# Two steps joined per turn of one TensorE loop, with the feed-forward weights and both query products loaded ahead of the attention steps

## The chip, the cores and the metric

One core of a Trainium2 chip, with float32 data throughout. The metric is the device time of one execution in microseconds; of the kernel before three runs are shown, with a median of 374.54 us. A core has five engines that run their own instruction streams: TensorE (PE in the profile; its weight loads are PEld), VectorE (DVE), ScalarE (ACT), GpSimd (POOL) and SyncE (SP). SP issues nearly all loads here; 16 DMA engines carry them out.

## The reference

One token of each of two sequences passes a layernorm, then an attention over a cache of 4096 positions and, beside it, a gated feed-forward; the product of both is added to the input.

```python
B, Sq, D = 2, 1, 448
Hq, Hkv, Sk, Dh = 16, 8, 4096, 256      # caches: (B, Hkv, Sk, Dh)
...
x = A_x
xn = _layernorm(x, axis=-1)
q = (xn @ wq) split into 16 heads; two query heads share one K/V head
s = softmax(q k^T / 16) v, joined over the heads, @ wo
g = silu(((xn w_gate) * (xn w_up)) @ w_down)     # F = 1792
return x + s * g
```

The caches are 2 x 67 MB and the weights some 24 MB, each read once; the output has 896 numbers.

## The kernel before, in words

A *step* is one K/V head of one sequence: 16 steps, numbered i = 2 x head + sequence. For each, K and V are 128 partitions x 8192 floats (4096 KB each). `scores` (lines 461-467) multiplies the query with K, `softmax` (503-505) takes the maximum over everything, the exponential and a transpose into `pT`, and `values` (516-521) multiplies it with V into the PSUM bank `o`.

Loads. There are two large buffers, `ring`, of 128 x 16384 floats, and one, `slot`, for weights (128 x 13440). `plan` lists the loads (lines 293-301) and `issue(n)` puts the next n on SP's queue (270-288). A ring load brings V of a step with K of the next (`vk[i]`, 8192 KB); a weight load brings wq0, then w_gate with w_up (`wgu`), w_down with wq1 (`wdq`), and `wo`. A load into a buffer that has been used waits on SP until TensorE has read the last of the old contents, and since SP issues in order, everything behind it waits too. What is issued is carried out in order.

Start. `issue(3)` on line 302 puts wq0 (with a small load wqx), K of step 0 and V0 with K1 in the queue with no wait. VectorE computes the layernorm and TensorE turns it into `xnT` and `xf`. `query(0)` (562) multiplies with wq0: `rows` (385-407) runs 12 matmuls over the first 384 rows of the weight, and for the last 64 rows of w_q half of the columns come in pieces, some of them from wqx, a tile of 16 partitions (`xeT`, lines 356-361, 397-405). All steps up to 6 are written out (568-581), and between them `ffn_in` (after step 1's softmax), `ffn_out` (step 3) and `query(1)` (step 4), each when its weights have come through the one slot.

Loop. Steps 6 to 13 are four turns of a loop on TensorE (`Flow.loop`, lines 119-149, and 203-207): TensorE's instructions of a turn are emitted once, and their waits become counting gates; the other engines' instructions are written out. In the second step of each turn `hold` (592-594) runs a 128x512 product twice that nobody reads.

Joining. Each step leaves `o` as four partial sums per head; `ob` keeps eight of them. `gather` sums the softmax totals (`total`) and the partial outputs (`combine`) with small matmuls, and `join` divides and transposes into `oT0` (steps 0-5, after step 5) and `oT1` (steps 6-13, after the loop). `project` multiplies with `wo`. The last two steps and the last part of wo, which comes behind V15 in the last loads, follow by hand (611-650).

`LEAD` (32, 154-155) is a number of semaphore increments on VectorE at the start that nobody waits for.

Of the kernel before, what the change touches and what calls it, by code (L numbers as in the profile page):

```python
# [4 lines left out]
AF = mybir.ActivationFunctionType  # L5
OP = mybir.AluOpType
# [14 lines left out]
GROUPS = 3  # L21
EARLY = 4 * GROUPS
LATE = 24
PART = 14 * (D + 512)
HALF = D - 384
SIDE = 16
COLS = 384
CUT = 256 + (512 - COLS) // 2
NS = HALF // SIDE
EPS = 1e-5  # L30
START = B * GROUPS
LEAD = 52
# [198 lines left out]
def gated_decode_block(nc, x, first, vk, last0, last1, wq0, wqx, wdq, wo, wgu, out):  # L231
# [7 lines left out]
    class Ring:  # L239
# [14 lines left out]
        ("mx", [1, NT, W], 1), ("ob", [128, 8, 512], 1))}  # L254
# [15 lines left out]
    def issue(n=1):  # L270
        for names, src, cuts in todo[:n]:
            weight = names[0].startswith("w")
            if weight:
                t = slot()
            else:
                t = ring()
            width = ROW if not weight else src.shape[1] // len(names)
# [6 lines left out]
            if names == ["wq0"]:  # L284
                at = src.shape[1]
                loaded["wqx"] = t[:SIDE, at:at + NS * COLS]
                SP.dma_start(loaded["wqx"], wqx[:, :4])
        del todo[:n]

    def plan(names, src, cuts=None):  # L290
        todo.append((names.split(), src, cuts or [0, src.shape[1]]))

    plan("wq0", wq0)
    plan("k0", first)
    weights = {0: ("wg wu", wgu), 2: ("wd wq1", wdq), 5: ("wo", wo)}
    for i in range(LAST):
        plan(f"v{i} k{i + 1}", vk[i])
        if i in weights:
            plan(*weights[i])
    plan(f"k{LAST + 1} v{LAST}", last0, [0, ROW, 2 * ROW])  # L300
    plan(f"v{LAST + 1} wo2", last1, [0, 6144, ROW, *(ROW + i * D for i in (5, 7, 8))])
    issue(3)
# [43 lines left out]

    oT1 = sbuf([128, HKV - 1 - GROUPS, 2, REP, W], "oT1")
    spare = oT1.rearrange("p g d r m -> p (g d r) m")

    xf = spare[:, NK:NK + 2]  # L350
# [4 lines left out]

    xeT = spare[:SIDE, NK + 2:NK + 2 + NS]
    pt = bank()
    for j in range(NS):
        at = 384 + j * SIDE
        PE.transpose(pt[:SIDE, B * j:B * (j + 1)], xn[:, at:at + SIDE], ident[:B, :B])  # L360
    copies(xeT, pt[:SIDE, :NS * B])

# [22 lines left out]
    def rows(ps, w, n, extra=None):  # L385
# [8 lines left out]
        def last(a, i):  # L394
            PE.matmul(ps[64 * a:64 * (a + 1), :n], xf.rearrange("p a j -> p (a j)"), block(i), start=False, stop=True)

        if extra is not None:
            last(1, 12)
            at = 13 * n
            PE.matmul(ps[W:2 * W, :CUT], xf[:, 0], w[:, at:at + CUT], start=False, stop=False)  # L400
            PE.matmul(ps[W:2 * W, CUT:n], xf[:, 1], w[:, at:at + n - CUT], start=False, stop=True)
            PE.matmul(ps[:W, COLS:n], xf[:, 1], w[:, at + n - CUT:at + CUT], start=False, stop=False)
            for j in range(NS):
                PE.matmul(ps[:W, :COLS], xeT[:, j, :], extra[:, j * COLS:(j + 1) * COLS], start=False, stop=j == NS - 1)
            return
        for a in range(2):
            last(a, 12 + a)
# [4 lines left out]
    def query(h):  # L412
        ps = bank()
        rows(ps, loaded[f"wq{h}"], 512, None if h else loaded["wqx"])
# [55 lines left out]
    su = sbuf([128, N], "su")  # L470

    def place(i):
        g, b = divmod(i, B)
        n = HKV - 1 - GROUPS
        return b * GROUPS + g if i < START else START + b * n + g - GROUPS if i < LAST else i

# [14 lines left out]
    def exponential(i, s, m, mx):  # L491
        sm = bank("sm")
        PE.transpose(sm[:, 128:129], mx.rearrange("p c j -> p (c j)"), one)
        DVE.tensor_scalar(m[:, 1:2], sm[:, 128:129], -1.0 / 16, None, op0=OP.mult)
        p = work["p"]()
        ACT.activation(p, s, AF.Exp, bias=m[:, 1:2], scale=1.0 / 16, accum_out=su[:, place(i):place(i) + 1])
        return p
# [9 lines left out]
    over = sbuf([128, N], "over")  # L507
    copy = Ring("qc", [128, 2, W], 2)

    def total(lo, hi, add):  # L510

        sm = bank("sm")
        PE.matmul(sm[:, :hi - lo], add.rearrange("p a r j -> p (a r j)"), su[:, lo:hi], start=True, stop=True)
        DVE.reciprocal(over[:, lo:hi], sm[:, :hi - lo])
# [8 lines left out]
    def combine(ob, n):  # L523

        cb = bank("cb")
        src = ob.rearrange("p s (e d c k) -> p s e d c k", e=2, d=2, c=NT)
        for e in range(2):
            for c in range(NT):
                PE.matmul(cb[W * c:W * (c + 1), :n * 64], add_blocks[:, e].rearrange("p r j -> p (r j)"),
                                 src[:, :n, e, :, c, :], start=e == 0, stop=e == 1)  # L530
        return cb

    def divide(cb, lo, hi):
        n = hi - lo
        t = work["h"]()
        DVE.tensor_tensor(t[:, :n * 64].rearrange("p (s k) -> p s k", s=n),
                                cb.rearrange("p (s k) -> p s k", s=n),
                                over[:, lo:hi, None].to_broadcast([128, n, 64]), op=OP.mult)
        return t[:, :n * 64]
# [5 lines left out]
    def turn(oT, cb, g, b, n):  # L545
        DVE.transpose(oT[:, g:g + n, :, :, DUP * b:DUP * (b + 1)].rearrange("p g d r j -> p (g d) r j"), cb)

    def heads(oT, i, first):
        return oT[:, i // 4 - first, i % 2, i % 4 // 2]

    def project(oT, first, lo, hi):
        for i in range(lo, hi):
            t = i % NT
            PE.matmul(wide[W * t:W * (t + 1), :D], heads(oT, i, first), loaded["wo"][:, i * D:(i + 1) * D],
# [9 lines left out]
    oT0 = sbuf([128, GROUPS, 2, REP, W], "oT0")  # L564
    oT2 = sbuf([128, 1, 2, REP, W], "oT2")
    s = scores(0, query_of(0), two())
    issue(2)
    for i in range(START):
        p = softmax(i, s)
        if i == 1:  # L570
            ffn_in()
        if i == 3:
            ffn_out()
        if i == 4:
            query(1)
        o = bank("o")
        values(i, p, o)
        s = scores(i + 1, query_of(i + 1), two())
        if i + 1 < START:
            issue(1 if i + 2 == START else 1 + (i + 1 in weights))  # L580
        DVE.tensor_copy(ob[:, place(i)], o)

    def gather(lo, hi):
        total(lo, hi, add_head)
        return combine(ob, hi - lo)

    def join(oT, cb, lo, hi):
        n = (hi - lo) // B
        for b in range(B):
            turn(oT, divide(cb[:, b * n * 64:(b + 1) * n * 64], lo + n * b, lo + n * (b + 1)), 0, b, n)  # L590

    def hold(p):

        PE.matmul(bank("cb"), ident, p[:, 0], start=True, stop=True)

    join(oT0, gather(0, START), 0, START)
    for first in range(START, LAST, 2):
        flow.turn = first
        issue(2)
        for i in (first, first + 1):  # L600
            p = softmax(i, s)
            if i > first:
                hold(p)
                hold(p)
            o = bank("o")
            values(i, p, o)
            DVE.tensor_copy(ob[:, place(i) - START], o)
            q = copy()
            ACT.copy(q, query_of(i + 1))
            s = scores(i + 1, q, two())  # L610
    flow.turn = None
    issue(2)
    m = peak(s)
    cb = gather(START, LAST)
# [3 lines left out]
    join(oT1, cb, START, LAST)  # L618
# [3 lines left out]
    project(oT0, 0, 0, EARLY)  # L622
    m = peak(late)
    project(oT1, GROUPS, EARLY, EARLY + NT)
# [6 lines left out]
    project(oT1, GROUPS, EARLY + NT, LATE)  # L631
    t = work["h"]()
    ACT.copy(t, wide[:, :D])
    total(14, 16, add_step)
    ACT.activation(ob[:, 6], o, AF.Copy, scale=over[:, 14:15])
# [5 lines left out]
    ACT.activation(ob[:, 7], o, AF.Copy, scale=over[:, 15:16])  # L641
    cb = combine(ob[:, 6:], B)
    DVE.transpose(oT2[:, 0].rearrange("p d r (b j) -> p b d r j", b=B), cb[:, :B * 64].rearrange("p (b d r j) -> p b d r j", b=B, d=2, r=REP))
    for i in range(LATE, NC):
        project_last(acc, heads(oT2, i, 7) if i >= 28 else heads(oT1, i, GROUPS), i)
# [55 lines left out]
```

## Time and profile before

| what | number |
|---|---|
| three runs | 374.32, 374.54, 374.59 us |
| profiled execution: span from first to last instruction | 373.3 us |
| median of the runs less that span | 1.24 us |
| TensorE busy | 201.8 us (54%) |
| VectorE busy | 74.1 us (20%) |
| ScalarE busy | 27.8 us (7%) |
| SP's load queue, share of 16 DMA engines | 98.5% |
| read from memory | 158.54 MB |

The profile does not give the profiled execution a time of its own beside its span, so the span is set against the median of the runs: 1.24 us lie outside of it.

How to read the rows: a timeline row has its start in us from the span's start, its length in us (for a row "x32" from the first instruction to the end of the last), engine, line, operation, tile written <- tiles read (buffer numbers left out), count, and in brackets how long the engine had been idle and who ended that. Every instruction passes through one helper, so all of them carry its line (L227 before, L220 in the change); they are told apart by their tiles. A 128x512 float32 matmul is two records, so "x32" are 16 matmuls. In a windows row, after the stretch and its length come the busy time and count of TensorE, the granted TensorE clock (1.00 is full), the busy share of the 16 DMA engines and the GB/s. A packet's whole share is put where it ended, so a short window can show more than 1.00. SPq rows are the issue of a DMA, not its transfer.

### The profile page before, as it was taken

To read this page: it belongs to the slowest core of one execution; us is meant where nothing else is said; L and a number is where in the kernel's file an instruction comes from. 1 tells how busy PE (TensorE), PEld (TensorE's weight loads), DVE (VectorE), ACT (ScalarE), POOL (GpSimd) and SP (SyncE) were. 2 spreads that over 40 slices of the span, in tenths; PEclk is the share of its full clock that TensorE was granted. 3 is DMA by queue.
4 is the path that set the end of the run, shared out by engine and by line. 5 is a ranking of instruction groups with operands and counts; after the bars stand their busy time and mean duration, and the time that the engine had idled before them with its cause. 6 is when DMAs were issued, how large, how long until landed. Compare 5 with 4: busy or idle time off the path is not lost. (4 is left out here: it accounts for less than half of the span.)

```text
span 373.3 us, 3175 instructions
## 1 busy us (share of the span) xinstructions
PE 201.8 (54%) x1416; PEld 58.6 (16%) x1416; DVE 74.1 (20%) x114; ACT 27.8 (7%) x52; POOL 2.4 (1%) x14
## 2 busy tenths in 40 slices
PE   0782449081736084817403667285609470948976
PEld 0220112020101021202100122022202120212223
DVE  2103040103030013030310212122211221030620
ACT  1101010001021001010100000101000101010120
POOL 0100000000000000000000000000000000000000
PEclk9988596677686589886955959686957896776999
DMA  8999999999999999999999999999999999999995
GB/s 329 437 471 400 444 457 435 421 437 400 444 427 428 451 435 430 428 426 433 449 428 428 435 449 409 442 449 421 435 421 449 435 428 442 435 393 432 442 406 240
DMA packets 3921, 158.73 MB, mean 425 GB/s; under 512 B 566, under 2 KB 696, under 8 KB 840
## 3 DMA queue, kind: packets, MB, share of 16 engines
q1 hardware_dynamic: 3908, 158.59, 98.5%
q8 instruction: 8, 0.13, 0.1%
q10 hardware_dynamic: 4, 0.00, 0.0%
q14 instruction: 1, 0.01, 0.0%
HBM read 158.54 MB, written 0.06 MB: 425 GB/s over the span
## 5 line engine op out<-in xcount | busy, mean ns | idle before, releaser
L227 PE MATMUL o<-ring,pT 128*32 128x512 f32 x480 | 76.6, 797 | 101.0 <-DMA ring<-vk 54.2
L227 PEld LDWEIGHTS o<-ring,pT 128*32 128x32 f32 x480 | 19.0, 142 | 153.5 <-issue 97.1
L227 DVE COPY ob<-o 128x512 f32<-128x512 f32 x14 | 9.7, 692 | 168.4 <-PE o L227 168.4
L227 ACT ACTIVATE p<-s,m 128x1024 f32<-128x1024 f32 x16 | 17.8, 1113 | 303.1 <-DVE m L227 303.1
L227 PE MATMUL s<-ring,qT 128*32 128x512 f32 x256 | 30.8, 622 | 1.1 <-DVE qT L227 1.1
L227 PE MATMUL s<-ring,qc 128*32 128x512 f32 x256 | 29.0, 592 | 0.0
L227 DVE TENSOR_REDUCE m<-s 128x1 f32<-128x1024 f32 x16 | 19.5, 1220 | 41.2 <-PE s L227 41.2
L227 DVE STREAM_TRANSPOSE pT<-p 128x1024 f32<-128x1024 f32 x15 | 18.7, 1245 | 19.1 <-ACT p L227 19.1
L227 PE MATMUL cb<-pT,ident 128*128 128x512 f32 x16 | 14.8, 1081 | 11.4 <-PEq L179 11.4
L227 PE MATMUL s<-slot,xnT 128*32 128x512 f32 (+1 forms) x96 | 14.6, 757 | 3.7 <-DMA slot<-wgu 3.7
L227 PE MATMUL sm<-ident,m 128*1 128x128 f32 x16 | 4.3, 270 | 21.0 <-PEq L179 12.9
L227 DVE TENSOR_REDUCE mx<-sm 1x128 f32<-1x512 f32 x16 | 10.9, 679 | 7.9 <-PE sm L227 7.9
L227 PEld LDWEIGHTS s<-ring,qc 128*32 128x32 f32 x256 | 9.0, 110 | 18.6 <-issue 18.6
L227 PEld LDWEIGHTS s<-ring,qT 128*32 128x32 f32 x256 | 8.2, 114 | 20.8 <-issue 20.7
L227 PE MATMUL sm<-one,mx 1*128 1x1 f32 x16 | 3.3, 209 | 12.3 <-PEq L179 6.9
L227 PE MATMUL s<-slot,hT 128*32 128x448 f32 x28 | 5.6, 911 | 4.4 <-DMA slot<-wdq 4.4
L227 PE MATMUL s<-slot,oT 16*32 16x384 f32 (+5 forms) x28 | 8.0, 521 | 0.0
L227 PEld LDWEIGHTS cb<-pT,ident 128*128 128x128 f32 x16 | 4.7, 324 | 15.8 <-issue 15.8
L227 PEld LDWEIGHTS sm<-ident,m 128*1 128x1 f32 x16 | 1.3, 79 | 34.8 <-issue 20.4
L227 PE MATMUL s<-ident,pT 2*128 2x2 f32 (+1 forms) x8 | 0.7, 203 | 10.7 <-DVE pT L227 10.7
L227 PEld LDWEIGHTS s<-slot,xnT 128*32 128x32 f32 x96 | 3.3, 137 | 12.9 <-issue 9.1
L227 PE MATMUL wide<-slot,oT 128*32 128x448 f32 x48 | 4.9, 539 | 0.0
(65 smaller groups left out, 58.2 us busy)
## 6 DMA issues: line engine op xcount, KB each, us to landing
ring<-last SPq DMA_DIRECT2D x2, 4096.0 KB, 26.7
slot<-wdq SPq DMA_DIRECT2D x1, 6720.0 KB, 45.6
slot<-wgu SPq DMA_DIRECT2D x1, 6272.0 KB, 33.7
slot<-wo SPq DMA_DIRECT2D x1, 5376.0 KB, 38.1
ring<-first SPq DMA_DIRECT2D x1, 4096.0 KB, 20.6
slot<-wq SPq DMA_DIRECT2D x1, 3488.0 KB, 11.2
ring<-last SPq DMA_DIRECT2D x1, 3072.0 KB, 21.4
ring<-last SPq DMA_DIRECT2D x1, 1120.0 KB, 24.1
```

The costliest lines, as they stand in the source:

```text
L227: self.flow.record(self.engine, lambda: method(out, *args, **kw), writes, reads, name == "dma_start")
```

## The change

Seven things change together.

- Loads: the order is now wq0 into ring buffer 1, wgu into the slot, wdq into ring buffer 0, K of step 0 behind wq0 in ring buffer 1 (`behind`), and these four are issued at once. V0 with K1 (ring buffer 0) and V1 with K2 (ring buffer 1) are issued with the first turn of the loop, and wo behind them.
- `ffn_in`, `ffn_out` and `query(1)` run straight behind `query(0)`, and the scores of step 0 behind them.
- The loop has seven turns, steps 0 to 13, instead of four.
- Each turn ends with the join of its two steps: `total`, `combine`, one division, one transpose. `oT0` and `oT1` become one tile `oT`, and `ob`, `su` and `over` hold two steps.
- `hold` goes.
- wqx goes: the last 64 rows of w_q are folded onto 128 partitions, as those of w_gate, w_up and wq1 already were, and `query(0)` ends with two 64-column matmuls. wq0 grows from 3488 to 3584 KB.
- `LEAD` is 0.

```diff
-    plan("wq0", wq0)
-    plan("k0", first)
-    weights = {0: ("wg wu", wgu), 2: ("wd wq1", wdq), 5: ("wo", wo)}
+    def behind():
+        return ring.bufs[1][:, WQ:]
+
+    plan("wq0", lambda: ring.bufs[1], wq0)
+    plan("wg wu", slot, wgu)
+    plan("wd wq1", lambda: ring.bufs[0], wdq)
+    plan("k0", behind, first)
     for i in range(LAST):
-        plan(f"v{i} k{i + 1}", vk[i])
-        if i in weights:
-            plan(*weights[i])
...
-    issue(3)
+        plan(f"v{i} k{i + 1}", ring, vk[i])
+        if i == 1:
+            plan("wo", slot, wo)
...
+    issue(4)
...
-        if extra is not None:
-            last(1, 12)
...
-            return
         for a in range(2):
-            last(a, 12 + a)
+            PE.matmul(ps[64 * a:64 * (a + 1), :n], xf.rearrange("p a j -> p (a j)"), block(12 + a), start=False, stop=True)
...
     query(0)
     ob = work["ob"]()
...
+    ffn_in()
+    ffn_out()
+    query(1)
     s = scores(0, query_of(0), two())
-    issue(2)
-    for i in range(START):
...
-    join(oT0, gather(0, START), 0, START)
-    for first in range(START, LAST, 2):
+    for first in range(0, LAST, B):
         flow.turn = first
         issue(2)
-        for i in (first, first + 1):
+        if first == 0:
+            flow.turn = None
+            issue()
+            flow.turn = first
+        for i in range(first, first + B):
             p = softmax(i, s)
-            if i > first:
-                hold(p)
-                hold(p)
             o = bank("o")
             values(i, p, o)
-            DVE.tensor_copy(ob[:, place(i) - START], o)
+            DVE.tensor_copy(ob[:, i % B], o)
             q = copy()
             ACT.copy(q, query_of(i + 1))
             s = scores(i + 1, q, two())
+        total(add_head)
+        cb = combine(ob)
+        t = work["h"]()[:, :B * 64]
+        DVE.tensor_tensor(t.rearrange("p (s k) -> p s k", s=B), cb.rearrange("p (s k) -> p s k", s=B),
+                          over[:, :, None].to_broadcast([128, B, 64]), op=OP.mult)
+        turn(oT, first // B, t)
     flow.turn = None
     issue(2)
     m = peak(s)
-    cb = gather(START, LAST)
```

The queue of SP before, from its start; `first` is K of step 0, `vk` a load of V and K, and a repeated form stands once with its count.

```order
L227 DMA slot<-wq 128x6976
L227 DMA slot<-wqx 16x1x1536
L227 DMA ring<-first 128x8192
L227 DMA ring<-vk 128x16384
L227 DMA slot<-wgu 128x12544
L227 DMA ring<-vk 128x16384 x2
L227 DMA slot<-wdq 128x13440
L227 DMA ring<-vk 128x16384 x3
```

The same place in the change:

```order
L220 DMA ring<-wq 128x7168
L220 DMA slot<-wgu 128x12544
L220 DMA ring<-wdq 128x13440
L220 DMA ring<-first 128x8192
L220 DMA ring<-vk 128x16384 x2
L220 DMA slot<-wo 128x10752
L220 DMA ring<-vk 128x16384 x12
```

The two weight loads moved ahead of K of step 0, and wdq from the slot into a ring buffer, so that the first `vk` load now comes behind it in the same buffer.

TensorE before, from step 3's transposes of the maximum to step 4's values: `s<-slot,hT` and `s<-h,add_head` are `ffn_out`, `s<-slot,xnT 32x512` with the row below it is `query(1)`, `o` rows are `values`, `s<-ring,qT` rows `scores`, and `sm` rows the transposes of the maximum.

```order
L227 MATMUL sm<-ident,m 1x128
L227 MATMUL sm<-one,mx 128x1
L227 MATMUL s<-slot,hT 32x448 x14
L227 MATMUL s<-h,add_head 32x112 x4
L227 MATMUL o<-ring,pT 32x512 x16
L227 MATMUL s<-ring,qT 32x512 x16
L227 MATMUL sm<-ident,m 1x128
L227 MATMUL sm<-one,mx 128x1
L227 MATMUL s<-slot,xnT 32x512 x12
L227 MATMUL s<-slot,oT_17 64x512 x2
L227 MATMUL o<-ring,pT 32x512 x16
```

The same products in the change, from `ffn_in`'s last rows to the first turn of the loop:

```order
L220 MATMUL s<-slot,oT 64x448 x2
L220 MATMUL s<-ring,hT 32x448 x14
L220 MATMUL s<-h,add_head 32x112 x4
L220 MATMUL s<-ring,xnT 32x512 x12
L220 MATMUL s<-ring,oT 64x512 x2
L220 MATMUL s<-ring,qT 32x512 x16
L198 UNCONDITIONAL_BRANCH
L220 MATMUL sm<-ident,m 1x128
L220 MATMUL sm<-one,mx 128x1
L220 MATMUL o<-ring,pT 32x512 x16
```

`ffn_out` and `query(1)` stand next to each other, both read the ring, and the scores of step 0 come behind them.

More of the change, by code (lines that the diff above doesn't have):

```diff
@@ L20 @@
 NC = HKV * 4
-GROUPS = 3
-EARLY = 4 * GROUPS
 LATE = 24
 PART = 14 * (D + 512)
[L25 to L29, printed above, removed]
 EPS = 1e-5
-START = B * GROUPS
-LEAD = 52
+WQ = 14 * 512
+LEAD = 0
 class Flow:
@@ L228, in __getattr__, with gated_decode_block @@
         return add
-def gated_decode_block(nc, x, first, vk, last0, last1, wq0, wqx, wdq, wo, wgu, out):
+def gated_decode_block(nc, x, first, vk, last0, last1, wq0, wdq, wo, wgu, out):
     flow = Flow(nc)
@@ L253, in gated_decode_block @@
         ("h", [128, D], 2), ("p", [128, 2, 512], 1), ("pT", [128, 2, 512], 1), ("m", [128, 2], 2),
-        ("mx", [1, NT, W], 1), ("ob", [128, 8, 512], 1))}
+        ("mx", [1, NT, W], 1), ("ob", [128, 2, 512], 1))}
     pairs = [nc.alloc_psum_tensor(f"s{i}", [128, 2, 512], F32)[:] for i in range(2)]
@@ L270, in issue @@
     def issue(n=1):
[L271 to L277, printed above, removed]
+        for names, place, src, cuts in todo[:n]:
+            t = place()
+            width = ROW if not names[0].startswith("w") else src.shape[1] // len(names)
             for i, name in enumerate(names):
@@ L283, in issue, with plan @@
                 SP.dma_start(t[:, lo:hi], src[:, lo:hi])
[L284 to L287, printed above, removed]
         del todo[:n]
-    def plan(names, src, cuts=None):
-        todo.append((names.split(), src, cuts or [0, src.shape[1]]))
-    plan("wq0", wq0)
-    plan("k0", first)
-    weights = {0: ("wg wu", wgu), 2: ("wd wq1", wdq), 5: ("wo", wo)}
-    for i in range(LAST):
-        plan(f"v{i} k{i + 1}", vk[i])
-        if i in weights:
-            plan(*weights[i])
-    plan(f"k{LAST + 1} v{LAST}", last0, [0, ROW, 2 * ROW])
-    plan(f"v{LAST + 1} wo2", last1, [0, 6144, ROW, *(ROW + i * D for i in (5, 7, 8))])
-    issue(3)
+    def plan(names, place, src, cuts=None):
+        todo.append((names.split(), place, src, cuts or [0, src.shape[1]]))
+    def behind():
[4 more added lines that the diff above has]
+    plan("k0", behind, first)
+    for i in range(LAST):
+        plan(f"v{i} k{i + 1}", ring, vk[i])
+        if i == 1:
+            plan("wo", slot, wo)
+    plan(f"k{LAST + 1} v{LAST}", ring, last0, [0, ROW, 2 * ROW])
+    plan(f"v{LAST + 1} wo2", ring, last1, [0, 6144, ROW, *(ROW + i * D for i in (5, 7, 8))])
+    issue(4)
     def early():
@@ L345, in gated_decode_block @@
     copies(xnT, pt[:, :(NK - 1) * B])
-    oT1 = sbuf([128, HKV - 1 - GROUPS, 2, REP, W], "oT1")
-    spare = oT1.rearrange("p g d r m -> p (g d r) m")
-    xf = spare[:, NK:NK + 2]
+    oT = sbuf([128, HKV - 1, 2, REP, W], "oT")
+    spare = oT.rearrange("p g d r m -> p (g d r) m")
+    xf = spare[:, :2]
     POOL.memset(xf, 0.0)
@@ L354, in gated_decode_block @@
         copies(xf[half, a:a + 1], pt[half, (NK - 1) * B:NK * B])
[L356 to L361, printed above, removed]
     both = work["h"]()[:B, :128].rearrange("p (c b j) -> p c b j", c=NT, b=B)
@@ L383, in gated_decode_block, with rows @@
     POOL.tensor_copy(add_blocks, rows4[:, :, :, None].to_broadcast([128, 2, REP, DUP]))
-    def rows(ps, w, n, extra=None):
+    def rows(ps, w, n):
         def block(i):
@@ L393, in rows @@
                 PE.matmul(ps[W * c:W * (c + 1), :n], xnT[:, k, :], block(NT * k + c), start=k == 0, stop=False)
-        def last(a, i):
-            PE.matmul(ps[64 * a:64 * (a + 1), :n], xf.rearrange("p a j -> p (a j)"), block(i), start=False, stop=True)
-        if extra is not None:
-            last(1, 12)
[L399 to L404, printed above, removed]
-            return
         for a in range(2):
-            last(a, 12 + a)
+            PE.matmul(ps[64 * a:64 * (a + 1), :n], xf.rearrange("p a j -> p (a j)"), block(12 + a), start=False, stop=True)
     qT = [sbuf([128, B, 4, 2, REP, DUP], "qT") for h in range(2)]
@@ L413, in query @@
         ps = bank()
-        rows(ps, loaded[f"wq{h}"], 512, None if h else loaded["wqx"])
+        rows(ps, loaded[f"wq{h}"], 512)
         for r in range(REP):
@@ L467, in scores @@
         return s
[L470 to L475, printed above, removed]
+    su = sbuf([128, B], "su")
     def peak(s):
@@ L495, in exponential @@
         p = work["p"]()
-        ACT.activation(p, s, AF.Exp, bias=m[:, 1:2], scale=1.0 / 16, accum_out=su[:, place(i):place(i) + 1])
+        ACT.activation(p, s, AF.Exp, bias=m[:, 1:2], scale=1.0 / 16, accum_out=su[:, i % B:i % B + 1])
         return p
@@ L505, in softmax, with total @@
         return turned(exponential(i, s, m, peak_of_all(m)), work["pT"]())
-    over = sbuf([128, N], "over")
+    over = sbuf([128, B], "over")
     copy = Ring("qc", [128, 2, W], 2)
-    def total(lo, hi, add):
+    def total(add):
         sm = bank("sm")
-        PE.matmul(sm[:, :hi - lo], add.rearrange("p a r j -> p (a r j)"), su[:, lo:hi], start=True, stop=True)
-        DVE.reciprocal(over[:, lo:hi], sm[:, :hi - lo])
+        PE.matmul(sm[:, :B], add.rearrange("p a r j -> p (a r j)"), su, start=True, stop=True)
+        DVE.reciprocal(over, sm[:, :B])
     def values(i, pT, o):
@@ L521, in values, with combine @@
                              loaded[f"v{i}"][:, e * 512:(e + 1) * 512], start=e < NT, stop=e >= KB - NT)
-    def combine(ob, n):
+    def combine(ob):
         cb = bank("cb")
@@ L528, in combine, with turn, heads, project @@
             for c in range(NT):
[L529 to L539, printed above, removed]
-    wide = bank("wide")
[L545 to L551, printed above, removed]
+                PE.matmul(cb[W * c:W * (c + 1), :B * 64], add_blocks[:, e].rearrange("p r j -> p (r j)"),
+                                 src[:, :, e, :, c, :], start=e == 0, stop=e == 1)
+        return cb[:, :B * 64]
+    def turn(oT, g, cb):
+        DVE.transpose(oT[:, g].rearrange("p d r (b j) -> p b d r j", b=B),
+                      cb.rearrange("p (b d r j) -> p b d r j", b=B, d=2, r=REP))
+    wide = bank("wide")
+    def heads(i):
+        return (oT if i < 28 else oT2)[:, i // 4 % 7, i % 2, i % 4 // 2]
+    def project(lo, hi):
         for i in range(lo, hi):
             t = i % NT
-            PE.matmul(wide[W * t:W * (t + 1), :D], heads(oT, i, first), loaded["wo"][:, i * D:(i + 1) * D],
+            PE.matmul(wide[W * t:W * (t + 1), :D], heads(i), loaded["wo"][:, i * D:(i + 1) * D],
                              start=i < NT, stop=i >= LATE - NT)
@@ L563, in gated_decode_block @@
     ob = work["ob"]()
-    oT0 = sbuf([128, GROUPS, 2, REP, W], "oT0")
     oT2 = sbuf([128, 1, 2, REP, W], "oT2")
+    ffn_in()
+    ffn_out()
+    query(1)
     s = scores(0, query_of(0), two())
-    issue(2)
-    for i in range(START):
[L569 to L594, printed above, removed]
-    join(oT0, gather(0, START), 0, START)
-    for first in range(START, LAST, 2):
+    for first in range(0, LAST, B):
         flow.turn = first
         issue(2)
-        for i in (first, first + 1):
+        if first == 0:
[3 more added lines that the diff above has]
+        for i in range(first, first + B):
             p = softmax(i, s)
-            if i > first:
-                hold(p)
-                hold(p)
             o = bank("o")
             values(i, p, o)
-            DVE.tensor_copy(ob[:, place(i) - START], o)
+            DVE.tensor_copy(ob[:, i % B], o)
             q = copy()
@@ L617, in gated_decode_block @@
     scores(LAST + 1, query_of(LAST + 1), late, (0,))
-    join(oT1, cb, START, LAST)
     p = exponential(LAST, s, m, mx)
@@ L621, in gated_decode_block @@
     ps = [turned(p, work["pT"]())]
-    project(oT0, 0, 0, EARLY)
+    project(0, 12)
     m = peak(late)
-    project(oT1, GROUPS, EARLY, EARLY + NT)
+    project(12, 16)
     mx = peak_of_all(m)
@@ L630, in gated_decode_block @@
     values(LAST, ps[0], o)
-    project(oT1, GROUPS, EARLY + NT, LATE)
+    project(16, LATE)
     t = work["h"]()
     ACT.copy(t, wide[:, :D])
-    total(14, 16, add_step)
-    ACT.activation(ob[:, 6], o, AF.Copy, scale=over[:, 14:15])
+    total(add_step)
+    ACT.activation(ob[:, 0], o, AF.Copy, scale=over[:, 0:1])
     o = bank()
@@ L640, in gated_decode_block @@
     spread(t, acc, True, False)
-    ACT.activation(ob[:, 7], o, AF.Copy, scale=over[:, 15:16])
-    cb = combine(ob[:, 6:], B)
-    DVE.transpose(oT2[:, 0].rearrange("p d r (b j) -> p b d r j", b=B), cb[:, :B * 64].rearrange("p (b d r j) -> p b d r j", b=B, d=2, r=REP))
+    ACT.activation(ob[:, 1], o, AF.Copy, scale=over[:, 1:2])
+    turn(oT2, 0, combine(ob))
     for i in range(LATE, NC):
-        project_last(acc, heads(oT2, i, 7) if i >= 28 else heads(oT1, i, GROUPS), i)
+        project_last(acc, heads(i), i)
     DVE.tensor_mul(gate, acc[:, :SL], gate)
@@ L679 @@
     wq0, wq1 = [folded(wq[:, h], 512) for h in range(2)]
-    t0, t1 = wq0[:HALF, 12 * 512:13 * 512], wq0[HALF:, 12 * 512:13 * 512]
-    wqx = np.zeros((SIDE // 4, 5, NS * COLS), np.float32)
-    wqx[:, :4] = t0[:, :COLS].reshape(NS, SIDE // 4, 4, COLS).transpose(1, 2, 0, 3).reshape(SIDE // 4, 4, NS * COLS)
-    half = np.concatenate([t1[:, :CUT], np.concatenate([t1[:, CUT:], t0[:, COLS:]], 1)])
-    wq0 = np.concatenate([wq0[:, :12 * 512], wq0[:, 13 * 512:], half], 1)
     wo = np.asarray(A_wo).reshape(NC, 128, D).transpose(1, 0, 2).reshape(128, NC * D)
@@ L693 @@
     nc = bacc.Bacc("TRN2", target_bir_lowering=False, num_devices=1, dynamic_dma_scratch_size=1024)
-    arrays = dict(x=x, first=first, vk=vk, last0=last[0], last1=last[1], wq0=wq0, wqx=wqx, wdq=wdq, wo=wo, wgu=wgu)
+    arrays = dict(x=x, first=first, vk=vk, last0=last[0], last1=last[1], wq0=wq0, wdq=wdq, wo=wo, wgu=wgu)
     args = [nc.dram_tensor(n, a.shape, mybir.dt.from_np(a.dtype), kind="ExternalInput").ap()
```

## Prediction

> **What bounds the kernel now.** I read the page first: the span, the strip of the DMA engines and the queues.
>
> ```profile
> span 373.3 us, 3175 instructions
> DMA  8999999999999999999999999999999999999995
> q1 hardware_dynamic: 3908, 158.59, 98.5%
> ```
>
> The 16 DMA engines are busy in every slice but the first and the last, and the queue that SP feeds takes 98.5% of their time. TensorE, at 54% on the same page, is no rival to that. The chain of waits in order of time says the same of the end: after the last wait of SP for TensorE there is only one long piece, the last load, and then 4.4 us of compute and store.
>
> ```profile
> 344.86 24.06 DMA ring<-last
> 368.96 2.06 PE s L227 x64
> ```
>
> Next I wanted the rate at which the queue is worked off. The timeline shows when TensorE is let go by successive loads: the end of the wait is the landing.
>
> ```profile
> 95.64 5.50 PE L227 MATMUL o<-ring,pT 128*32 128x512 f32 x32 [8.44 <-DMA ring<-vk]
> ...
> 111.58 5.62 PE L227 MATMUL s<-slot,hT 128*32 128x448 f32 x28 [4.39 <-DMA slot<-wdq]
> ...
> 130.89 4.94 PE L227 MATMUL o<-ring,pT 128*32 128x512 f32 x32 [12.47 <-DMA ring<-vk]
> ```
>
> Between the first and the last of these lie the 6720 KB of wdq and one 8192 KB load of V and K (128 x 16384 floats), 15.27 MB in 35.25 us: 433 GB/s. I use this rate throughout: 8192 KB take 19.4 us, 4096 KB 9.7 us. All 158.59 MB at it take 366.2 us, so the kernel is its transfers, plus a few microseconds before them and behind them. A change can help only at those two ends, and it hurts wherever it lets the queue run empty.
>
> The list of DMA issues, with the timeline's issue times, gives the front end.
>
> ```profile
> slot<-wdq SPq DMA_DIRECT2D x1, 6720.0 KB, 45.6
> slot<-wgu SPq DMA_DIRECT2D x1, 6272.0 KB, 33.7
> ...
> ring<-first SPq DMA_DIRECT2D x1, 4096.0 KB, 20.6
> slot<-wq SPq DMA_DIRECT2D x1, 3488.0 KB, 11.2
> ...
> slot<-wqx SPq DMA_DIRECT2D x1, 96.0 KB
> res<-gate SPq DMA_DIRECT2D x1, 56.0 KB, 1.6
> ```
>
> ```profile
> 0.74 0.39 SPq L227 DMA_DIRECT2D slot<-wq  x1
> 1.19 0.79 SPq L227 DMA_DIRECT2D slot<-wqx  x1
> 2.04 0.40 SPq L227 DMA_DIRECT2D ring<-first  x1
> 2.48 0.53 SPq L227 DMA_DIRECT2D ring<-vk  x1
> ...
> 23.09 0.33 SPq L227 DMA_DIRECT2D slot<-wgu  x1
> ...
> 42.03 5.00 PE L227 MATMUL o<-ring,pT 128*32 128x512 f32 x32 [9.93 <-DMA ring<-vk]
> ```
>
> The first load lands at 0.74 + 11.2 = 11.94 us. Its 3.57 MB need 8.25 us, so it acts as if data had flowed at full rate from 3.69 us on; call that the origin. K of step 0 lands at 22.64 us with 7.86 MB (18.16 us) before it: origin 4.48. The origin moved by 0.79 us between the two, where only wqx was added. It then stays: 130.89 us with 54.7 MB behind it gives 4.5. So before has no hole in its queue from 23 us to the end, and the reason stands in the rows: at the first wait of SP, 16.25 MB were queued, good until 42 us, and the next load was issued at 23.09.
>
> **What the change moves at the front.** After it, SP issues four loads without a wait: wq0 (now 3584 KB), wgu (6272), wdq (6720) into ring buffer 0, and K of step 0 (4096) behind wq0 in ring buffer 1. The next, V0 with K1, overwrites ring buffer 0, so SP holds it until TensorE has read all of wd and all of wq1, that is until the end of ffn_out and query(1). Behind that wait on SP stand V1 with K2, wo and every later load. Before, the same load was issued at 2.48 us and waited for nothing.
>
> Landing of wdq: 16576 KB are 16.97 MB, 39.2 us at the rate; from the origin 3.69 (no wqx) 42.9 us. K of step 0 lands 9.7 us later, at 52.6. This is all the cover there is: from 42.9 us TensorE has 9.7 us for two products whose price before shows in other places.
>
> ```profile
> 117.25 0.62 DVE L227 COPY h<-s 128x448 f32<-128x448 f32 x1 [7.36 <-PE s L227]
> ...
> 118.03 0.40 PE L227 MATMUL s<-h,add_head 128*32 128x112 f32 x8 [0.82 <-DVE h L227]
> ...
> 141.81 2.78 PE L227 MATMUL s<-slot,xnT 128*32 128x512 f32 x24
> ...
> 144.53 1.08 PE L227 MATMUL s<-slot,oT 128*64 128x512 f32 x4
> ```
>
> From the landing of wdq at 111.58 the first product ran to 117.2, VectorE lifted the result, and the four spreading matmuls ended at 118.43: 6.85 us. query(1) ran from 141.81 to 145.61: 3.80 us. In the new order nothing stands between the two on TensorE, so wdq's landing to SP's release takes 10.65 us, 10.7 with SP's own step. V0 with K1 is issued at 42.9 + 10.7 = 53.6 us, a microsecond after the last byte of the queue has landed. That is the hole.
>
> How wide it is depends on what a load costs that is issued on an empty queue, from issue to its origin. Before has two such: the first load, 2.95 us (0.74 to 3.69), and the store at the end, 1.6 us less 0.13 for its bytes, 1.47 us. The first is large like ours but has the start of the program in it; the store is small. I take the middle, 2.2. The delay against an unbroken queue is then 53.6 + 2.2 - 52.6 = 3.2 us.
>
> The Trainium skill speaks against the change here too: "DMA: Bandwidth & Descriptors", section "Anatomy of one DMA", puts about 2.0 us of fixed cost on every DMA (measured on another issuing path), and it is hidden only while something else is queued. By that figure the delay would be 3.0 us, an estimate; the trace's 1.47 and 2.95 lie on both sides of it.
>
> The part of 10.7 us that may differ is TensorE's speed. The table of windows gives the granted clock as ffn_out and one of the value products ran.
>
> ```profile
> 44.00:45.00 1.00, 1.00 (x8) 0.59 0.58 251
> 45.00:46.00 1.00, 1.00 (x12) 1.00 1.27 552
> ...
> 115.00:116.00 1.00, 1.00 (x8) 0.50 1.06 459
> 116.00:117.00 1.00, 1.00 (x8) 0.75 1.21 524
> ...
> 118.00:119.00 1.00, 0.40 (x8) 1.00 0.30 131
> 119.00:120.00 1.00, 0.00 (x0) 0.96 1.51 655
> 120.00:122.00 2.00, 0.00 (x0) 0.50 1.01 434
> ```
>
> The clock is 0.50 when work begins after a pause. In ffn_out it rose at about 116.5, 4.9 us after the start; in the value product that began at 42.03 at about 44.8, 2.8 us after. In the new order TensorE also comes to ffn_out from a pause. ffn_in shows its length here, from its first matmul to the transpose that makes hT:
>
> ```profile
> 56.81 4.71 PE L227 MATMUL s<-slot,xnT 128*32 128x448 f32 x24 [3.73 <-DMA slot<-wgu]
> ...
> 66.62 0.65 DVE L227 STREAM_TRANSPOSE hT<-h 128x448 f32<-128x448 f32 x1
> ```
>
> That is 10.5 us. wgu will land at 27.0 us (10.09 MB, 23.3 us behind the origin), so hT is ready by 38 and TensorE then waits for wdq. Were the clock to rise after 2.8 us, 2.1 us at half speed would become 1.05 and the chain 9.65 us. Were it to fall again in the pause for the lift, query(1) would run like query(0):
>
> ```profile
> 13.76 4.62 PE L227 MATMUL s<-slot,xnT 128*32 128x512 f32 x24
> ```
>
> 4.62 us against 2.78, and with the two wide products about 2 us more in all. I keep 10.7, the row that is ffn_out itself.
>
> "TensorE: Matmul & The Clock Gate", part 1, of the Trainium skill puts the slow stretch at one free-running window of about 3.4 us. By that ffn_out would be 0.75 us shorter than its row and the delay 2.45 us, an estimate; the row, at 4.9, is longer than one such window.
>
> **What the change removes.** wqx and its load go, its bytes are in wq0. The origin should then stay at 3.69: a gain of at most 0.79 us, at least nothing, since two landings are all I have for it. I take 0.79. The small matmuls of query(0), four transposes and a copy go with it; they lie under the wait for loads and bring nothing.
>
> **The loop.** All 14 steps now run in seven turns, and each turn ends with total, combine, a product and a transpose for two steps; the two idle products ("hold") go. One place before shows such a join between two steps.
>
> ```profile
> 170.04 5.84 PE L227 MATMUL o<-ring,pT 128*32 128x512 f32 x32 [7.92 <-DMA ring<-vk]
> 175.71 3.61 PE L227 MATMUL s<-ring,qT 128*32 128x512 f32 x32
> ...
> 179.39 51.60 SPq L227 DMA_DIRECT2D ring<-vk  x3
> ...
> 186.72 1.25 DVE L227 STREAM_TRANSPOSE pT<-p 128x1024 f32<-128x1024 f32 x1 [1.27 <-ACT p L227]
> ```
>
> The ring's buffer is free when the scores end: SP issues the next load at 179.39, 9.35 us after the landing, while the load in flight lasts 19.4 us. The join comes behind that on TensorE, so it can't hold SP. It delays the next softmax; pT is done 17.9 us after the landing even with a join of six steps, still ahead of the next landing. If that cover of 1.5 us were gone, the value product would start late, and only a lateness of over 10 us would empty the queue. I cost the loop at nothing, and so too the loss of hold: a value product all at the low clock is a microsecond or two longer, against those 10. V1 with K2 needs the scores of step 0, some 4 us behind query(1), under the 19.4 us of V0 with K1. At the end the same pieces of the last load land last and the same work follows; the join of 8 steps that leaves the end lay under the last loads.
>
> **The sum.** The profiled execution has a span of 373.3 us; the median of the runs, 374.54, is 1.24 above it, and I carry that over. Delay 3.2, less 0.79 for wqx: +2.4 us, span 375.7, time 376.9 us. With 9.65 us and 1.47 it is +0.6 (375.1); with 10.7, 2.95 and no gain from wqx +3.95 (378.5).
>
> **The rivals.** *The cover holds, and it is not slower.* K of step 0 hides the two products if the chain and the cost of an empty queue together stay under 9.7 us. This needs TensorE at full clock from the landing of wdq: the 4.9 us at half clock become 2.45, the chain 8.2 us, and with 1.47 the sum is just 9.7. Only wqx's gain is left: 373.75 to 374.5 us. Against it stand the rows in which the clock is 0.50 after a wait for a load, and the wait for wdq would be a long one; for it, that landings are by the slowest of 16 engines, so that the others' share of V0 with K1 might start under K's tail.
>
> *query(1) is slow too.* The pause of a microsecond for the lift lets the clock fall, or the clock never rises in ffn_out. The chain is 12.7 us and the time 378.9 us, up to 380.5 with the upper costs. For it: in ffn_out the clock was low for nearly all of it. Against: from 118 to 119 us, right behind the lift, the clock was full, and it fell only at about 120, 1.5 us after the last spreading matmul; the lift's pause is 0.8.
>
> **How the numbers follow.** I give the forecast 0.72, the cover 0.15, the slow query(1) 0.13. A measurement of this kernel can tell about 0.2% from no change, 0.75 us. The forecast's own range is 375.1 to 378.5, with 0.05 of its chance inside the 0.75; the cover's case is split, 0.08 no change and 0.07 faster. So faster 0.07, same 0.05 + 0.08 = 0.13, slower 0.67 + 0.13 = 0.80. The range reaches to the upper edge of the cover's case and into the slow query's: 374.8 to 379.2.
>
> **What would show it.** In the profile after, SP's first wait should be for query(1), with V0 with K1 issued at 52 to 54 us; the DMA share in the windows from 52 to 56 us should fall well under one, for 2 to 4 us in sum, and nowhere else before the end. TensorE should wait for V0 with K1 until about 75 us. K of step 0 should land at about 52.6; if wdq and it land 0.8 later, wqx cost nothing. The forecast is wrong if the load is issued before 50 us, if the share shows no dip, or if a dip shows in the loop.

## The result and the profile after

The changed kernel takes 378.98 us (median of 4 runs, 377.86 to 379.56) against 374.43 before: a ratio of 1.0114, 95% interval 1.0092 to 1.0136, 4.5 us slower. The forecast was 376.9, within 374.8 to 379.2. The profiled execution took 379.15 us, with a span of 377.8.

The page after, in the lines that answer to those of before: the strip of the DMA engines now has a weak place in its sixth slice (47 to 57 us), and the queue's share fell by one point.

```profile
span 377.8 us, 3298 instructions
DMA  8999979999999999899999999999999999989995
GB/s 340 474 437 410 412 281 430 402 397 437 433 476 444 444 430 423 382 438 444 444 437 444 444 437 444 430 409 395 444 444 444 437 444 444 437 389 406 435 421 233
q1 hardware_dynamic: 3888, 158.59, 97.5%
```

TensorE and SP around that place, from the timeline after: ffn_out, the lift, query(1), the scores of step 0, and the issue of V0 with K1 and V1 with K2.

```profile
44.08 5.52 PE L220 MATMUL s<-ring,hT 128*32 128x448 f32 x28 [8.36 <-DMA ring<-wdq]
49.65 0.62 DVE L220 COPY h<-s 128x448 f32<-128x448 f32 x1 [12.58 <-PE s L220]
...
50.61 2.78 PE L220 MATMUL s<-ring,xnT 128*32 128x512 f32 x24
...
53.32 1.08 PE L220 MATMUL s<-ring,oT 128*64 128x512 f32 x4
54.33 3.64 PE L220 MATMUL s<-ring,qT 128*32 128x512 f32 x32
54.44 3.92 SPq L220 DMA_DIRECT2D ring<-vk  x2
```

From the landing of wdq to SP's issue are 10.4 us. The list of DMA issues has K of step 0 landing 51.4 us after its issue at 2.11, at 53.5 us, 0.9 us before V0 with K1 is issued.

```profile
2.11 0.59 SPq L220 DMA_DIRECT2D ring<-first  x1
```

```profile
ring<-first SPq DMA_DIRECT2D x1, 4096.0 KB, 51.4
ring<-wq SPq DMA_DIRECT2D x1, 3584.0 KB, 11.0
```

Windows of a microsecond over the same place show what the engines did (TensorE's busy time, its clock, then the DMA share and the GB/s).

```profile
50.00:51.00 1.00, 0.58 (x12) 1.00 1.21 524
51.00:52.00 1.00, 1.00 (x16) 1.00 0.08 33
52.00:53.00 1.00, 1.00 (x16) 1.00 0.00 0
53.00:54.00 1.00, 1.00 (x8) 1.00 0.00 0
54.00:55.00 1.00, 1.00 (x10) 1.00 0.00 0
55.00:56.00 1.00, 1.00 (x12) 1.00 2.91 983
```

A packet is a piece of a load that one engine moves. Its whole share stands in these rows where it began, and not where it ended, as the explanation of the rows at the start has it. The row from 55 to 56 shows this: its 983 KB are 15 packets of 64 KB, which at a share of 2.91 took 3.1 us each, and packets of a load that was issued at 54.44 can't have run for 3.1 us and be over by 56.00. So a row without bytes is one in which no packet begins, and the ends are read from the packet records of the trace: 15 of the 16 engines end K of step 0 between 51.25 and 51.78 us, and one, which began its last packet at 51.92, at 53.13. The landing is reported at 53.5, when that one is through. The first packets of V0 with K1 begin at 55.40, 0.96 us after the issue. For about four microseconds nearly all engines stand empty, and this is the hole.

Behind it little is lost. In the loop after, the value products of steps 0, 1, 3, 5 and 13 begin, each at the landing of its load:

```profile
76.33 5.19 PE L220 MATMUL o<-ring,pT 128*32 128x512 f32 x32 [15.60 <-PEq L172]
...
96.94 5.13 PE L220 MATMUL o<-ring,pT 128*32 128x512 f32 x32 [9.23 <-PEq L172]
...
148.21 5.09 PE L220 MATMUL o<-ring,pT 128*32 128x512 f32 x32 [6.87 <-PEq L172]
...
186.82 6.26 PE L220 MATMUL o<-ring,pT 128*32 128x512 f32 x32 [7.45 <-PEq L172]
...
341.64 5.66 PE L220 MATMUL o<-ring,pT 128*32 128x512 f32 x32 [8.14 <-PEq L172]
```

Eight loads lie between the last two, 19.35 us each, and 19.4 is what 8192 KB take at 433 GB/s. Only the second load behind the hole is late once more: it lands 20.6 us after the first (96.94 against 76.33). At step 6 the changed kernel is 4.0 us behind (206.14 against 202.11 before), and at the first piece of V15 4.6 us (368.41 against 363.81); from there to the end of the span are 9.4 and 9.5 us. So nearly all of the difference of 4.5 us in the span is there before the loop is half done; the half microsecond that comes later is not traced to a cause.

### The profile page after: what moved, and what is told of

Same layout as the page of the kernel before. It is cut to its first block, busy times and chain, and to the rows that moved or that the text cites. A ratio compares the mean times of both kernels' runs of the same rounds, so it can differ in the third digit from the quotient of the medians.

```text
span 377.8 us, 3298 instructions
## 1 busy us (share of the span) xinstructions
PE 189.9 (50%) x1474; PEld 57.6 (15%) x1474; DVE 75.5 (20%) x124; ACT 28.6 (8%) x58; POOL 2.4 (1%) x14
## 5 line engine op out<-in xcount | busy, mean ns | idle before, releaser
L220 PE MATMUL o<-ring,pT 128*32 128x512 f32 x480 | 82.4, 848 | 118.2 <-PEq L172 118.2
L220 PE MATMUL s<-ring,qc 128*32 128x512 f32 x448 | 50.7, 592 | 0.0
L220 PEld LDWEIGHTS o<-ring,pT 128*32 128x32 f32 x480 | 20.8, 149 | 167.2 <-issue 167.2
L220 PEld LDWEIGHTS s<-ring,qc 128*32 128x32 f32 x448 | 15.1, 110 | 33.2 <-issue 33.2
L220 PE MATMUL s<-slot,xnT 128*32 128x448 f32 x48 | 7.2, 748 | 7.4 <-DMA slot<-wgu 7.4
L220 PE MATMUL s<-ring,hT 128*32 128x448 f32 x28 | 5.5, 903 | 8.4 <-DMA ring<-wdq 8.4
L220 PE MATMUL s<-ring,xnT 128*32 128x512 f32 x48 | 8.1, 825 | 0.0
L220 PE MATMUL s<-ring,qT 128*32 128x512 f32 x64 | 7.5, 597 | 0.0
L220 PE MATMUL s<-ident,pT 2*128 2x2 f32 x4 | 0.6, 246 | 10.7 <-DVE pT L220 10.7
L220 PE MATMUL cb<-ob,add_blocks 128*32 128x128 f32 x128 | 5.2, 279 | 0.6 <-ACT ob L220 0.6
L220 PEld LDWEIGHTS sm<-one,mx 1*128 1x128 f32 x16 | 2.3, 142 | 16.6 <-issue 15.7
L220 PE MATMUL s<-ring,slot 128*32 128x512 f32 x32 | 3.6, 596 | 1.1 <-DMA ring<-last 1.1
## 6 DMA issues: line engine op xcount, KB each, us to landing
ring<-first SPq DMA_DIRECT2D x1, 4096.0 KB, 51.4
```

The lines of the kernel that those rows point to most:

```text
L220: self.flow.record(self.engine, lambda: method(out, *args, **kw), writes, reads, name == "dma_start")
```

## The experiments

The theory: all of the loss is the empty queue at 51 to 55 us, and its size is the time at which SP may issue V0 with K1. The rivals: the hole is only a part and the loop's joins or the loss of hold the rest; or a restart has a fixed price, whatever its width.

**wo ahead of V0 with K1.** The slot is free once ffn_in is through, so the load of wo can stand in the queue while query(1) still runs.

```diff
     plan("k0", behind, first)
+    plan("wo", slot, wo)
...
-        if i == 1:
-            plan("wo", slot, wo)
...
     ffn_in()
+    issue()
     ffn_out()
     query(1)
...
-        if first == 0:
-            flow.turn = None
-            issue()
-            flow.turn = first
```

> The changed kernel with wo issued ahead of V0 with K1, as soon as ffn_in has read the slot (about 36 us), so that 12.7 us of transfer stand behind K of step 0 while query(1) still runs. Theory (all of the loss is the one hole in the load queue while SP waits for query(1)): no hole, TensorE gets V0 with K1 about 12.7 us later than it would without any hole, and the time falls by the whole 4.5 us to 374.4, plus or minus 0.5. Rival A (the hole explains only the 3.2 us that the prediction gave it, the rest comes from the joins in the loop or from hold being gone): 375.5 to 376.2. Rival B (the hole has little to do with it): 378 to 379.

Measured: 374.12 us, ratio to before 0.9993 (0.9985 to 1.0002). The whole loss is gone, with the seven-turn loop, the joins, the folded piece and no hold all still in. V0 with K1 is issued no sooner than in the changed kernel, but wo stands in the queue in the meantime:

```profile
34.96 0.33 SPq L220 DMA_DIRECT2D slot<-wo  x1
...
54.51 60.57 SPq L220 DMA_DIRECT2D ring<-vk  x4
```

```profile
50.00:51.00 1.00, 0.52 (x12) 1.00 1.21 524
51.00:52.00 1.00, 1.00 (x14) 1.00 1.57 678
52.00:53.00 1.00, 1.00 (x16) 1.00 0.99 430
53.00:54.00 1.00, 1.00 (x11) 1.00 0.60 258
54.00:55.00 1.00, 1.00 (x12) 1.00 1.59 688
55.00:56.00 1.00, 1.00 (x16) 1.00 0.10 43
```

A packet counts where it begins, so single windows swing; over these six microseconds the share has a mean of 1.01, where the changed kernel had 0.70. Both rivals fall. That this version beats the kernel before is not shown: the interval holds 1.

**The folded piece alone, in the kernel before.**

```diff
-            if names == ["wq0"]:
-                at = src.shape[1]
-                loaded["wqx"] = t[:SIDE, at:at + NS * COLS]
-                SP.dma_start(loaded["wqx"], wqx[:, :4])
...
-        rows(ps, loaded[f"wq{h}"], 512, None if h else loaded["wqx"])
+        rows(ps, loaded[f"wq{h}"], 512)
```

> The kernel before with w_q's last rows folded onto 128 partitions alone: wqx and its load go, wq0 has 3584 KB. The prediction gave this 0.79 us: 373.7. Theory now (the origin of the transfers rises by about 1 us over the first 40 us with or without wqx, since in the changed kernel it went from 3.3 to 4.8 us without it): no change, 374.4 plus or minus 0.3.

Measured: 374.26 us, ratio 1.0000 (0.9986 to 1.0013). The interval reaches to a gain of 0.5 us, so the 0.79 of the prediction is refuted. In its trace the list of issues has

```profile
slot<-wgu SPq DMA_DIRECT2D x1, 6272.0 KB, 36.8
...
slot<-wq SPq DMA_DIRECT2D x1, 3584.0 KB, 11.0
```

with wgu issued at 20.07: the origin, worked out as in the prediction, is 0.74 + 11.0 - 8.48 = 3.3 us at wq0 and 56.87 - 52.37 = 4.5 us at wgu. It rises by 1.2 us with no small load in the queue, so wqx is not needed for it. The trace also has what rises: each load brings 16 semaphore increments, and the landing is the last of them. The 16 of wq0 lie between 11.24 and 11.72 us; of those of wgu, 14 lie between 55.07 and 55.51, and the last two come at 56.18 and 56.82. By the first 14 the origin is still 3.1 us (55.51 - 52.37). Two engines have fallen behind, and the landing is theirs. In the changed kernel it is the same with wdq: 15 increments between 41.88 and 42.39 us, and the last at 44.03.

**A sixth of wo ahead of V0 with K1**, the rest where wo was. The issue behind ffn_in is as in the first run, the one in the loop's first turn stays:

```diff
+    plan("wo", slot, wo, [0, 1792])
...
         if i == 1:
-            plan("wo", slot, wo)
+            plan("wrest", lambda: slot.bufs[0][:, 1792:NC * D - 8 * D], wo[:, 1792:])
```

> The changed kernel with only the first sixth of wo (896 KB, 2.1 us of transfer) issued ahead of V0 with K1, the rest where wo was. Theory of one hole: the hole shrinks by these 2.1 us and no more, so 376.7 to 377.1. If the loss is a fixed price of restarting the queue, whatever the width of the hole: 378.5 to 379. If the time came from elsewhere than the hole: 379.

Measured: 377.08 us, ratio 1.0066 (1.0049 to 1.0082): 1.9 us better than the changed kernel for 2.1 us of transfer. The hole was not closed (15 of the 16 increments of the sixth of wo come by 54.47 us, the first packets of V0 with K1 begin at 54.95), and yet the time fell by about what was filled of it, so the loss is not one fixed price of a restart, whatever the width. That a constant part stands beside the width is not excluded by this run.

**TensorE kept at full clock before ffn_out.**

```diff
     ffn_in()
+    for i in range(8):
+        PE.matmul(bank("cb"), ident, loaded["wq0"][:, :512], start=True, stop=True)
     ffn_out()
```

> The changed kernel with eight 128x512 products that nobody reads between ffn_in and ffn_out, so that TensorE comes to ffn_out without a pause and at full clock. Theory: ffn_out takes about 3.0 us in place of 5.5, SP's wait for query(1) ends about 2.4 us earlier, the hole is that much narrower: 376.4 to 376.9. Rival (the hole's width is not set by TensorE): 379.

Measured: 376.23 us, ratio 1.0049 (1.0036 to 1.0063). The lines of its timeline for ffn_out, the issue of V0 with K1, and the scores, which now wait for K of step 0:

```profile
43.63 3.20 PE L220 MATMUL s<-ring,hT 128*32 128x448 f32 x28 [0.21 <-DMA ring<-wdq]
...
51.68 5.63 SPq L220 DMA_DIRECT2D ring<-vk  x2
53.28 3.64 PE L220 MATMUL s<-ring,qT 128*32 128x512 f32 x32 [1.64 <-DMA ring<-first]
```

The granted clock is 1.00 in every window from 43 to 47 us. ffn_out takes 3.20 us in place of 5.52 and begins 0.45 us earlier, since wdq landed that much sooner in this execution; the issue comes 2.76 us earlier (51.68 against 54.44), and the time falls by 2.75. The load is now issued 1.6 us before K of step 0 has landed, and there still is a loss of 1.8 us: the landing of the last load is not the moment at which the queue runs empty.

**ffn_out's products twice.**

```diff
-        for i in range(14):
+        for i in range(28):
+            i %= 14
             t = i % NT
```

> The changed kernel with ffn_out's 14 products run twice over (the second time they start the sums anew, so the result stays). 14 products at full clock are 14 x 0.19 = 2.7 us more before SP may issue V0 with K1. Theory (every microsecond of SP's wait for query(1) is a microsecond of the time): 378.98 + 2.7 = 381.7, plus or minus 0.5. Rival (the price of the hole is a restart of fixed size, or later loads catch up): under 380.

Measured: 381.69 us, ratio 1.0200 (1.0182 to 1.0218).

```profile
57.16 3.92 SPq L220 DMA_DIRECT2D ring<-vk  x2
```

The issue is 2.72 us later than in the changed kernel, and the time 2.71 us longer. With the run before this one the three points (51.68, 376.23), (54.44, 378.98) and (57.16, 381.69) lie on a line of slope one. The times are medians of four to six runs, which spread over 0.7 to 1.8 us in each kernel.

**The kernel before without hold.**

```diff
             p = softmax(i, s)
-            if i > first:
-                hold(p)
-                hold(p)
```

> The kernel before without hold, the product that is run twice in each turn and read by nobody. Theory (the loop has 10 us to spare in each step): no change, 374.4 plus or minus 0.3. Rival (hold keeps TensorE's clock up and so the ring's buffers come free in time): 375.5 or more.

Measured: 374.47 us, ratio 1.0003 (0.9992 to 1.0013). In the kernel before, hold is worth half a microsecond at most, either way.

**A hole in the kernel before**, with nothing else of the change.

```diff
     plan("k0", first)
-    weights = {0: ("wg wu", wgu), 2: ("wd wq1", wdq), 5: ("wo", wo)}
+    plan("wg wu", wgu)
+    weights = {2: ("wd wq1", wdq), 5: ("wo", wo)}
...
-    issue(3)
+    issue(2)
...
     s = scores(0, query_of(0), two())
-    issue(2)
+    issue(3)
```

> The kernel before with one thing moved: V0 with K1 stands in SP's queue behind wgu, and wgu waits for query(0), whose products end about 23.1 us, 0.45 us after K of step 0 has landed. Nothing of the change's loop, join or weights is in it. Theory (an empty queue costs about 3.5 us counted from the landing of the last load to the issue of the next, as in the changed kernel and in the run with TensorE kept warm): 0.45 + 3.5 = 4.0 us, 378.4, plus or minus 0.5. The prediction's 2.2 us would give 377.0. Rival (the change's loss has another source than the empty queue): 374.4 to 375.

Measured: 379.41 us (378.28 to 380.34), ratio 1.0142 (1.0124 to 1.0161), 4.6 to 6.0 us slower than before. So the kernel before loses as much from one hole as the change lost; but it was expected at 4.0, plus or minus 0.5, and was larger. In the profiled execution, the fastest of the four at 378.28 us, wgu was issued at 22.53, and K of step 0 landed at 2.03 + 20.8 = 22.83:

```profile
2.03 0.41 SPq L227 DMA_DIRECT2D ring<-first  x1
22.53 0.33 SPq L227 DMA_DIRECT2D slot<-wgu  x1
```

```profile
20.00:21.00 1.00, 1.00 (x4) 1.00 0.38 164
21.00:22.00 1.00, 1.00 (x4) 1.00 0.08 33
22.00:23.00 1.00, 0.50 (x2) 1.00 0.00 0
23.00:24.00 1.00, 0.39 (x4) 0.71 2.43 753
```

Here too 15 engines are through with K before its landing, between 20.27 and 21.59 us, and the last at 22.36; the price against the landing is 3.7 + 0.3 = 4.0 us. Why the other three runs took up to 2 us more was not settled. The issue follows the end of query(0), at 22.50 us here and 23.06 in the trace of the kernel before; whether this end moves enough from run to run to explain the spread is not shown.

## Why the prediction was right, and by how much it was off

**The mechanism was right.** The queue ran empty once, in front of V0 with K1, because SP held that load for query(1); the loop, the joins and hold cost nothing that the runs show. The run with wo ahead and the two runs that moved the issue by 2.7 us either way show it.

**The landings and the chain were right within 1.3 us.** wdq was put at 42.9 us and came at 44.05, K of step 0 at 52.6 and came at 53.5, the chain at 10.7 and was 10.4, the issue at 53.6 and was 54.44, the landing of V0 with K1 at about 75 and was 76.33. wdq and K of step 0 came about a microsecond late, which the prediction had named as the sign that wqx cost nothing.

**The step that failed is the price of an empty queue, 2.2 us, and with it the 0.79 us for wqx; they are one mistake.** The prediction took the origin after the first landing, 3.69 us, as the price of a start (2.95 us), and put the later rise to 4.48 down to wqx. The rise is there without wqx: it is one or more engines falling behind the rest. Taken whole, the start's price is 4.48 - 0.74 = 3.74 us from issue to a settled origin. With it, and nothing for wqx, the prediction's own sum reads: K of step 0 at 4.48 + 48.89 = 53.4, the issue at 4.48 + 39.20 + 10.7 = 54.4, the delay 54.4 + 3.74 - 53.4 = 4.7 us, the time 379.3; measured were 4.5 and 378.98. What the runs give for the price, counted from the landing of the last load to the issue of the next, is the loss less that distance: 4.55 - 0.9 = 3.6 us in the changed kernel, 1.8 + 1.6 = 3.4 with TensorE warm, 7.14 - 3.66 = 3.5 with ffn_out twice, 2.7 + 1.7 = 4.4 behind the sixth of wo (landed at 55.7, the next issued at 54.0), 4.0 in the kernel before with a hole. All are above both bounds that the prediction set, 1.47 and 2.95. The small store at the end was no measure for it, and the first landing was read too early.

Up to the landing of V0 with K1 the 2.2 was in fact close: 76.33 less 19.4 us for its bytes and less the issue at 54.44 are 2.5 us. The rest, 1.2 us, came one load later, in the 20.6 us to the landing of V1 with K2: the 16 increments of V0 with K1 lie within 0.5 us (75.67 to 76.19), and of the next load's one comes 1.3 us behind the other 15 (96.80 against 95.49).

**In part it was luck that the range held.** The forecast's own terms reach 378.5 at most, and 378.98 lies above that. The range went up to 379.2 for the sake of a slow query(1), which did not come.

**Why the price is so high** shows in the packet records. In the changed kernel an engine stood idle for 4.05 us on the mean, from the end of its last packet of K (51.56) to its first packet of V0 with K1 (55.61), and these first packets of 64 KB took 3.07 us in place of the 2.44 us of the next ones. Together that is 4.7 us, and the profiled execution, 379.15 us, lies 4.7 above 374.43. The same count gives 1.9, 7.4 and 3.4 us with TensorE warm, with ffn_out twice and in the kernel before with a hole, where the profiled executions lost 1.6, 7.1 and 3.7.

Counted from the landing of the last load to the issue of the next, the price in the changed kernel has three parts. The landing waits for the slowest engine, 2.0 us behind the mean. The first packets begin 0.96 us after the issue, and 1.2 us on the mean. And they take 0.6 us longer than the next ones. Where something is queued behind, an engine that is done goes on with that: in the run with wo ahead, wo's first packets begin at 51.24 us, while the slowest engine's last packet of K runs to 52.95.

"DMA: Bandwidth & Descriptors", section "Anatomy of one DMA", of the Trainium skill says, for another issuing path, that most of a DMA's fixed cost of about 2.0 us is the confirmation of the last bytes. The trace does not agree with that for these loads: from the end of K's last packet (53.13) to the landing (53.52) are 0.4 us, and the price of the hole was 3.4 to 4.4.

**The first rival** (TensorE at full clock, no loss) was tried as a run: at full clock ffn_out takes 3.20 us, and 1.8 us of loss stay. The chain is then 8.05 us, as that rival had it, but with a price of 3.4 us it doesn't fit under the cover of 9.7. That rival's remark on engines which are done early, and so might start on V0 with K1 under K's tail, did not come true in the changed kernel, where nothing was there for them to start on; with TensorE warm it did, as 14 engines begin on it between 52.65 and 53.09 us, before K lands at 53.2. **The second** (query(1) slow) did not come: query(1) took 3.79 us at full clock, right behind the lift.

**Left open:** why one or more engines fall behind the others, and what sets the spread in the last run.

## What to carry to other kernels

Where a kernel is its transfers, ask of each load which instruction lets it go, and how many bytes stand queued at that moment; the reserve has to cover the compute and, by these runs, 3.4 to 4.4 us more, since most engines are idle before the last landing is seen, and the next load's packets begin late and slowly. A load that is late for its buffer need not leave the queue empty: another that needs no such buffer can go ahead of it, as wo did here. And the price of a start is read from landings some loads later, when the lag has settled, and not from the first one.

## What the runs showed of the hardware that was not expected

- A load's landing is that of its slowest engine. In the changed kernel 15 of the 16 engines ended K of step 0 between 51.25 and 51.78 us, the last at 53.13, and the landing came at 53.5; in the kernel before with a hole they ended between 20.27 and 21.59, the last at 22.36, and the landing came at 22.83.
- The lag of landings behind the bytes moved grows by about 1.2 us over the first 40 us of a queue (3.3 to 4.5 us), with or without a small load in it. One or more engines fall behind; with w_q folded, the lag by the other 14 is still 3.1 us.
- On an empty queue the first packets began 0.95 to 0.97 us after the issue in four traces, and where they had 64 KB they took 3.0 to 3.1 us on the mean in place of 2.4.
- ffn_out from a pause took 5.52 us, and with TensorE kept busy before it 3.20; it stands in front of SP's release, and these 2.3 us are the larger part of the 2.75 us by which the kernel's time fell.
